# Routed expert layer: rows of two of four tiles transposed by PE, first product in two halves through three single PSUM banks, logits' bank emptied by ACT

## The chip, the cores and the metric

One core of one Trainium2 chip runs the whole program. The metric is the device time of one execution in microseconds; several executions are taken and their median counts. One further execution was recorded by the profiler, and all rows below come from it.

## The reference, cut to what matters

Three stages follow one another on 24,576 tokens (8 x 3072) of 256 channels.

```python
# 1. spectral filter along the sequence
Y = np.fft.rfft(x, axis=1) * (filt_r + 1j * filt_i)[None]
x = np.fft.irfft(Y, n=3072, axis=1).reshape(24576, 256)
# 2. routed experts, E = 8, F = 1024: each token goes through the one expert with the largest logit
for e in range(8):
    xe = x[expert_idx == e]
    out[expert_idx == e] = gate_w * (np.maximum(xe @ w1[e], 0) @ w2[e])
# 3. soft slots: 8 experts with 4 slots each
logits = out @ phi                      # 24576 x 32
d = softmax(logits, axis=0)             # over tokens
slot_input = d.T @ out                  # 32 x 256
slot_out = experts(slot_input)          # relu(s @ w1[e]) @ w2[e], 4 slots per expert
y = softmax(logits, axis=1) @ slot_out
```

## The kernel before, in words

The program has three parts that follow each other on the chip. The spectral filter (to about 760 us of the profiled span) also writes every token's row, scaled and split into two fp16 parts (high and low, 512 numbers in all) with some bookkeeping words, to a table `xd` in HBM that is sorted by expert. The routed experts (761 to 1594 us) read this table in tiles of 128 rows of one expert; there are `NT` = 199 tiles. The tail (1594 to 1718 us) works out the slots and writes the output.

The change is in the middle part, `moe_phase`. Each tile `t` passes these steps, and each engine gets them in an order that is written out by hand in `ORDER`, one loop iteration per tile, with lags (`XC` = 4 tiles, `LA` = 3, `LG` = 11):

- `load`: a DMA on ACT's queue brings the 128 rows into `mx` (line 820), six iterations ahead. Four buffers.
- `xpose`, four iterations ahead: GpSimd copies the bookkeeping words to `meta`. For tiles 0 and 1 (`PEX` = 2) PE transposes the rows by four 128x128 transposes into a PSUM tile `px`, and ACT copies it to `mxp`. For all others DVE copies the rows to `xg` (line 847), and once a pair of tiles (`XG` = 2) stands there, a DMA transpose on SP's queue writes `mxt` (line 851). Two buffers of a pair each.
- `gemm1` (line 855): 12 matmuls of 512 columns give `ph` = rows times w1 of the tile's expert, 128 x 1024 in two PSUM banks, two such buffers. The matmuls alternate between the two halves of 512 columns. ACT takes the ReLU of all 1024 columns as fp16 (line 871), then DVE takes the rest that fp16 leaves (line 872); both go to `h`. A DMA transpose on SP's queue writes `ht` (line 874).
- `l2` (line 883), three iterations later: 16 small matmuls add the tile's slot logits to `pl2`, one PSUM bank that holds the logits of four tiles (a group). There is one such bank, so the next group's first tile needs it emptied.
- `c_sum` (line 899), in the iteration after the group's last `l2`: DVE copies one half of `pl2` out (line 902) and adds the other (line 903). `c_logits`, `c_max`, `c_state`, `c_comb1`, `c_comb2`, `c_weights`, `c_low`, `c_den` follow in later iterations and make the running softmax over tokens and the softmax over slots.
- `gmm`, eleven iterations later: 8 small matmuls into a PSUM tile `pg` (two buffers), which `gacc` on DVE adds to an accumulator.

In one iteration PE's stream is: the small matmuls of the group steps, `gemm1` of tile t, `l2` of tile t-3, `gmm` of tile t-11. After the `gemm1` of every fourth tile, ahead of `l2`, PE's sequencer loads the expert numbers of the next four tiles (line 868).

PSUM has eight banks: `ph` takes four, `pg` two, `pl2` and `tr` one each.

`M1A` = 7 tiles of 512 KB of the slot experts' w1 are loaded into `m1a` during the middle part; the other 9 of 16 into `m1b` at the start of the tail (line 1087).

Of the kernel before, what the change touches and what calls it, by code (L numbers as in the profile page):

```python
# [9 lines left out]
F32 = mybir.dt.float32  # L10
F16 = mybir.dt.float16
# [3 lines left out]
AF = mybir.ActivationFunctionType  # L15
ALU = mybir.AluOpType
# [8 lines left out]
F = 1024  # L25
NS = 32
# [5 lines left out]
NT = NTOK // 128 + 7  # L32
# [3 lines left out]
R = 12  # L36
CH = 2
NEG = -1.0e30
M1A = 7
WA, WQ = 6, "G"  # L40
KW = 112
CROSS = 2
# [4 lines left out]
ENDS = (3, 3)  # L47
PF, XC, XG, XEN, XQN, XB, MEN = 6, 4, 2, "V", "SC", 4, "G"
PGB = 2
PEX = 2  # L50
LAX = 3
LGX = 8
ORDER = [('load', 0), ('weights', 4), ('state', 3), ('max', 2), ('sum', 1), ('logits', 1), ('low', 4), ('comb1', 2), ('comb2', 3), ('gacc', 0), ('den', 4), ('w2copy', 0), ('mref', 0), ('xpose', 0), ('gemm1', 0), ('l2', 0), ('gmm', 0)]
# [131 lines left out]
def build(ctx, tc, A, out):  # L185
    nc = tc.nc
    V, SC, G, PE, SY = nc.vector, nc.scalar, nc.gpsimd, nc.tensor, nc.sync
# [16 lines left out]
    w1s = cp.tile([128, E, 2, 2, F], F16, tag="big", name="w1s")  # L204
# [575 lines left out]
    def moe_phase(ctx):  # L780
        mp = ctx.enter_context(tc.tile_pool(name="mp", bufs=2))
        ps = ctx.enter_context(tc.tile_pool(name="ps2", bufs=1, space=PSUM))
# [10 lines left out]
        LG = LA + LGX  # L793
        XE, XQ = dict(V=V, G=G, SC=SC)[XEN], dict(SC=SC, SY=SY)[XQN]
        xgs = {}
        rows_, xts, metas, hs, hts, w2c, pl2s, grp, pgs, es = {}, {}, {}, {}, {}, {}, {}, {}, {}, {}


        regs = {}
# [1 line left out]
        def fetch(eng, g, f):  # L801
            if g >= NG or (id(eng), g, f) in regs:
                return
            n = min(4, NT - 4 * g)
            p, j = divmod(4 * g % 128, 32)
            _, vs = nc.values_load_multi_w_load_instructions(
                tab[p:p + 1, f, 4 * g // 128, j:j + n], engines=[eng.engine], min_val=0, max_val=(E - 1, DUMMY)[f],
                skip_runtime_bounds_check_because=why)
            regs[id(eng), g, f] = vs

        def val(eng, j, f):
            fetch(eng, j // 4, f)
            return regs[id(eng), j // 4, f][j % 4]
# [10 lines left out]
        def xpose(t):  # L824
            if t >= NT:
                return
            x = rows_.pop(t)
            g, q = divmod(t, 4)
            if q == 0:
                metas[g] = mp.tile([128, 4, 4], F32, tag="meta", name=f"meta{g}", bufs=6)  # L830
            (V if MEN == "V" else G).tensor_copy(metas[g][:, q, :], x[:, 512:PITCH].bitcast(F32))
            if t == NT - 1 and q < 3:
                V.memset(metas[g][:, q + 1:], 0.0)
                V.memset(metas[g][:, q + 1:, 1:2], NEG)
            if t < PEX:

                px = ps.tile([128, 4, 128], F16, tag="pg", name=f"px{t}", bufs=PGB)
                for k in range(4):
                    PE.transpose(px[:, k, :], x[:, k * 128:k * 128 + 128].bitcast(F16), id16)
                xt = mp.tile([128, 4, 128], F16, tag="xt", name=f"mxp{t}", bufs=2)  # L840
                SC.copy(xt, px)
                xts[t] = xt
                return
            g, q = divmod(t, XG)
            if q == 0:
                xgs[g] = mp.tile([128, XG, 512], F16, tag="xg", name=f"xg{g}", bufs=2)
            (XE.copy if XE is SC else XE.tensor_copy)(xgs[g][:, q, :].bitcast(U16), x[:, 0:512])
            if q == XG - 1 or t == NT - 1:
                xg = xgs.pop(g)
                xt = mp.tile([128, XG * 4, 128], F16, tag="xt", name=f"mxt{g}", bufs=2)  # L850
                SY.dma_start_transpose(out=xt[:, 0:4 * q + 4], in_=xg[:, 0:q + 1].rearrange("p a f -> p (a f)"))
                for i in range(q + 1):
                    xts[t - q + i] = xt[:, 4 * i:4 * i + 4]

        def gemm1(t):
            e = val(PE, t, 0)
            ph = ps.tile([128, F], F32, tag="ph", name=f"ph{t}", bufs=2)
            xt = xts.pop(t)
            n = [0, 0]
            for k in range(2):  # L860
                for part, ws in ((0, (0, 1)), (1, (0,))):
                    for w in ws:
                        for hf in range(2):
                            PE.matmul(ph[:, hf * 512:hf * 512 + 512], xt[:, 2 * part + k, :],  # L864
                                      w1s[:, ds(e, 1), k, w, hf * 512:hf * 512 + 512].rearrange("p a f -> p (a f)"),
                                      start=(n[hf] == 0), stop=(n[hf] == 5))
                            n[hf] += 1
            if t % 4 == 2:
                fetch(PE, t // 4 + 1, 0)
            h = mp.tile([128, 2, F], F16, tag="h", name=f"h{t}", bufs=LG + 2)  # L870
            SC.activation(h[:, 0, :], ph, AF.Relu)  # L871
            V.scalar_tensor_tensor(out=h[:, 1, :], in0=ph, scalar=0.0, in1=h[:, 0, :], op0=ALU.max, op1=ALU.subtract)  # L872
            ht = mp.tile([128, 16, 128], F16, tag="ht", name=f"ht{t}", bufs=LA + 1)
            SY.dma_start_transpose(out=ht, in_=h.rearrange("p a f -> p (a f)"))
            hs[t], hts[t] = h, ht
# [7 lines left out]
        def l2(t):  # L883
            g, q = divmod(t, 4)
            if q == 0:
                pl2s[g] = ps.tile([128, 4, 2 * NS], F32, tag="pl2", name=f"pl2_{g}")
            ht, w = hts.pop(t), w2c.pop(t)
            for k in range(8):
                PE.matmul(pl2s[g][:, q, :], ht[:, k, :], w[:, k, :], start=(q == 0 and k == 0), stop=False, skip_group_check=True)  # L889
                PE.matmul(pl2s[g][:, q, 0:NS], ht[:, 8 + k, :], w[:, k, 0:NS], start=False, stop=((q == 3 or t == NT - 1) and k == 7),  # L890
                          skip_group_check=True)

        n4 = [128, 4, NS]
        b4 = lambda v: v.unsqueeze(2).to_broadcast(n4)
# [4 lines left out]
        def c_sum(g):  # L899
            a = n4t("a", g)  # L900
            m = min(4, NT - 4 * g)
            V.tensor_copy(a[:, 0:m], pl2s[g][:, 0:m, NS:])
            V.tensor_tensor(out=a[:, 0:m], in0=a[:, 0:m], in1=pl2s[g][:, 0:m, 0:NS], op=ALU.add)
            if m < 4:
                V.memset(a[:, m:], 0.0)
            grp[g] = dict(a=a)
# [125 lines left out]
        for t in range(XC):  # L1032
            xpose(t)
            if t + XB < PF:
                load(t + XB)
        for t in range(NT + LG + 2):
            if t >= 16 and t % 8 == 0 and t < 16 + 8 * M1A:
                SY.dma_start(m1a[:, t // 8 - 2, :], w21[t // 8 - 2])
            if t == NT:
                w, get = weights("moe_w2", C, "w2n")  # L1040
                w2n.extend(w)
                get(SY, range(WA))
            ops = dict(weights=c_weights, state=c_state, max=c_max, sum=c_sum, logits=c_logits, low=c_low, comb1=c_comb1, comb2=c_comb2,
                       den=c_den)
            one = dict(gacc=(gacc, LG + 1), w2copy=(w2copy, LA - 1), mref=(mref, LG), xpose=(xpose, -XC), gemm1=(gemm1, 0), l2=(l2, LA), gmm=(gmm, LG), load=(load, -PF))
            for n_, lag in ORDER:
                if n_ in one:
                    at(t, one[n_][0], one[n_][1])
                else:
                    grp_at(t, ops[n_], lag)  # L1050
# [20 lines left out]
    def weights(src, n, nm):  # L1071
        w = cp.tile([128, E, A[src].shape[1] // 128, n], F32, tag="big", name=nm)
        return [w[:, e] for e in range(E)], lambda q, es: [
            q.dma_start(w[:, e], A[src][e].rearrange("(k p) c -> p k c", p=128)) for e in es
        ]

    w2n = []
    m1a = cm.tile([128, M1A, F], F32, tag="m1a", name="m1a")
    w21 = A["moe2_w1"].rearrange("e (k p) f -> (e k) p f", p=128)


    def tail(ctx):
        tp = ctx.enter_context(tc.tile_pool(name="tp", bufs=1))
        ps = ctx.enter_context(tc.tile_pool(name="ps3", bufs=1, space=PSUM))
        m1b = tp.tile([128, 2 * E - M1A, F], F32, tag="big", name="m1b")
        for i in range(M1A, 2 * E):
            SY.dma_start(m1b[:, i - M1A, :], w21[i])
        m1 = [m1a[:, i] if i < M1A else m1b[:, i - M1A] for i in range(2 * E)]
        M = sm.tile([128, 1], F32, tag="M", name="M")
# [123 lines left out]
    with ExitStack() as c3:  # L1213
        moe_phase(c3)
# [31 lines left out]
```

## Time and profile before

| | us |
|---|---|
| median of 3 executions | 1716.07 (1710.61 to 1718.2) |
| the profiled execution, its own time | 1719.86 |
| its span, first to last instruction | 1718.1 |
| PE busy | 1449.7 (84% of the span) |
| DVE busy | 1203.3 (70%) |
| ACT busy | 784.7 (46%) |
| GpSimd busy | 636.9 (37%) |

The profiled execution took 3.8 us more than the median of the others, and 1.8 us of its time lie outside the span. A matmul's end is modelled in these rows, so that several matmuls overlap; the distance between two starts tells how fast PE goes. The idle time printed with a group is what its engine lay idle just before its instructions, and the arrow names what ended the wait.

### The profile page before, as it was taken

The page shows a single profiled execution, that of the slowest core. Times are in us where ns is not written, and L with a number is a line of the kernel's source. Part 1 is how long each engine was busy: PE and PEld are TensorE (multiplying, and loading weights), DVE is VectorE, ACT ScalarE, POOL GpSimd, SP SyncE. Part 2 cuts the span into 40 slices and gives each one's busy share as a digit, 9 for nine tenths or more (in the row PEclk, how much of TensorE's full clock was granted, in tenths as well). Part 3 has the DMA queues.
Part 4 walks back from the last instruction along what each step waited for, and adds up shares of the span by engine and source line. Part 5 has one row for each costly group of instructions (what it writes and reads, how often), then busy time and mean ns, then how long its engine had stood idle before and what let it go on. Part 6 is the DMA issues. An engine that isn't in the chain of part 4 may idle for free.

```text
span 1718.1 us, 35843 instructions
## 1 busy us (share of the span) xinstructions
PE 1449.7 (84%) x10761; PEld 682.8 (40%) x10761; DVE 1203.3 (70%) x3053; ACT 784.7 (46%) x1816; POOL 636.9 (37%) x877
## 2 busy tenths in 40 slices
PE   6768779988888876648999989999999999997876
PEld 2222224333444433324444444544444444443332
DVE  0377779999999955445677777877777777776134
ACT  3355436554666655423444444444444444443133
POOL 1122224665566644531333333333333333334200
PEclk9898989999999987769999999999999999997899
DMA  8999989997878665439999999999999999999999
GB/s 284 296 318 309 288 263 298 292 280 221 252 241 250 207 220 186 160 113 207 205 212 227 202 201 207 211 202 200 211 199 197 207 200 203 204 200 249 337 313 376
DMA packets 720696, 405.72 MB, mean 236 GB/s; under 512 B 554561, under 2 KB 658896, under 8 KB 720512
## 3 DMA queue, kind: packets, MB, share of 16 engines
q1 hardware_dynamic: 634560, 295.09, 77.4%
q10 hardware_dynamic: 69824, 77.52, 15.2%
q0 software_dynamic: 16128, 30.83, 5.5%
q8 instruction: 95, 1.56, 0.4%
q14 instruction: 89, 0.73, 0.1%
HBM read 164.60 MB, written 105.52 MB: 157 GB/s over the span
## 4 chain that ended last, share of the span: by engine, by line
PE 38%; DVE 23%; DMA 17%; ACT 9%; issue 8%; another core or an unknown queue 3%; ACTq 1%; SPq 1%; POOL 0%; DVEq 0%
PE ph L864 13%; DVE h L872 5%; DMA ht<-h 5%; ACT h L871 4%; PE p L440 3%; PE U L363 3%; PE W L331 2%; DVE rows L468 2%; DMA vd<-vo 2%; PE pl L889 2%; PE p L307 2%; DMA zd<-zo 2%; PE pg L1000 2%; DMA mxt<-xg 2%
## 5 line engine op out<-in xcount | busy, mean ns | idle before, releaser
L864 PE MATMUL ph<-w1s,mxt 128*128 x2364 | 547.4, 381 | 10.2 <-DMA mxt<-xg 6.7
L864 PEld LDWEIGHTS <-mxt 128*128 128x128 f16 x2364 | 232.4, 101 | 264.2 <-issue 26.1
L872 DVE SCALAR_TENSOR_TENSOR h<-ph,h 128x1024 f16<-128x1024 f32 x199 | 243.2, 1222 | 123.4 <-ACT h L871 106.9
L871 ACT ACTIVATE h<-ph 128x1024 f16<-128x1024 f32 x199 | 203.5, 1022 | 163.6 <-PE ph L864 115.1
L404 POOL DMA_INDIRECT xd<-rows,dest x192 | 189.5, 987 | 160.2 <-ACT xT L478 51.7
L388 POOL TENSOR_TENSOR t<-t,t 112x512 f32<-112x512 f32 x112 | 142.0, 1271 | 251.8 <-DVE t L385 237.1
L935 POOL DMA_INDIRECT cd<-cr,meta x199 | 196.9, 989 | 62.4 <-issue 47.2
L363 PE MATMUL U<-zi,mt 96*128 96x512 f32 x256 | 146.6, 657 | 41.2 <-issue 20.3
L889 PE MATMUL pl<-w2c,ht 128*128 128x64 f16 x1592 | 114.9, 190 | 44.7 <-DVE fl L911 21.9
L331 PE MATMUL W<-t,mt 112*96 112x512 f32 x288 | 151.1, 617 | 0.8 <-ACT vo L332 0.8
L889 PEld LDWEIGHTS <-ht 128*128 128x128 f16 x1592 | 101.9, 97 | 83.6 <-issue 37.5
L307 PE MATMUL p<-xt,cs 128*128 128x512 f32 x192 | 114.1, 689 | 21.4 <-DMA xt<-in_x 11.6
L440 PE MATMUL p<-vt,cs 128*128 128x512 f32 x192 | 113.5, 675 | 18.1 <-DVE rows L468 17.9
L890 PE MATMUL pl<-w2c,ht 128*128 128x32 f16 x1592 | 112.2, 178 | 0.0
L478 ACT COPY xT<-tr 128x1024 f16<-128x1024 f16 x96 | 97.0, 1010 | 29.1 <-remote 16.2
L462 ACT ACTIVATE rows<-p,r 128x256 f16<-128x256 f32 x192 | 80.6, 472 | 64.4 <-DVE r L459 38.2
L332 ACT COPY vo<-W 96x512 f32<-96x512 f32 x128 | 74.4, 581 | 71.1 <-PE W L331 50.6
L890 PEld LDWEIGHTS <-ht 128*128 128x128 f16 x1592 | 95.5, 96 | 25.2 <-issue 12.2
L1015 DVE TENSOR_TENSOR acc<-acc,pg 128x512 f32 x149 | 101.6, 682 | 1.5 <-PE pg L1004 0.7
L309 ACT COPY zo<-p 128x512 f32<-128x512 f32 x96 | 55.9, 582 | 93.7 <-PE p L307 51.6
L380 DVE TENSOR_TENSOR t<-U,w2s 112x512 f32<-112x512 f32 x128 | 87.8, 686 | 15.5 <-PE U L363 6.9
L477 PEld LDWEIGHTS <-rows 128*128 128x128 f16 x768 | 56.2, 105 | 93.6 <-issue 93.6
(246 smaller groups left out, 2151.5 us busy)
## 6 DMA issues: line engine op xcount, KB each, us to landing
mx<-xd ACTq DMA_DIRECT2D x199, 130.0 KB
xt<-in_x SPq DMA_DIRECT2D x96, 256.0 KB
zd<-zo ACTq DMA_DIRECT2D x96, 256.0 KB
zi<-zd SPq DMA_DIRECT2D x128, 192.0 KB
vd<-vo ACTq DMA_DIRECT2D x128, 192.0 KB
vt<-vd SPq DMA_DIRECT2D x96, 256.0 KB
out_y<-ot SPq DMA_DIRECT2D x48, 512.0 KB
w2s<-in_ff SPq DMA_DIRECT2D x93, 96.0 KB
```

Source lines behind the costliest of these rows:

```text
L307: PE.matmul(p, cs1[:, 0:128], xt[:, 2 * m:2 * m + 2, :], start=True, stop=True)
L331: PE.matmul(W, mt[:, 128 + 96 * i:224 + 96 * i], t, start=(i == 0), stop=(i == len(ts) - 1))
L363: PE.matmul(U, mt[0:96, 0:128], zi, start=True, stop=True)
L388: G.tensor_tensor(out=t1, in0=t1, in1=t2, op=ALU.add)
L404: i = G.indirect_dma_start(out=xd, out_offset=bass.IndirectOffsetOnAxis(ap=dest[:, t:t + 1], axis=0), in_=rows[:, t % 2, :].bitcast(U16), ...
L440: PE.matmul(p, cs1[:, 128:256], vt[:, 2 * i % CH:2 * i % CH + 2, :], start=True, stop=True)
L864: PE.matmul(ph[:, hf * 512:hf * 512 + 512], xt[:, 2 * part + k, :], w1s[:, ds(e, 1), k, w, hf * 512:hf * 512 + 512].rearrange("p a f -> p ...
L871: SC.activation(h[:, 0, :], ph, AF.Relu)
L872: V.scalar_tensor_tensor(out=h[:, 1, :], in0=ph, scalar=0.0, in1=h[:, 0, :], op0=ALU.max, op1=ALU.subtract)
L889: PE.matmul(pl2s[g][:, q, :], ht[:, k, :], w[:, k, :], start=(q == 0 and k == 0), stop=False, skip_group_check=True)
L890: PE.matmul(pl2s[g][:, q, 0:NS], ht[:, 8 + k, :], w[:, k, 0:NS], start=False, stop=((q == 3 or t == NT - 1) and k == 7), skip_group_check= ...
L935: i = G.indirect_dma_start(out=cd, out_offset=bass.IndirectOffsetOnAxis(ap=metas[g].bitcast(U32)[:, q, 2:3], axis=0), in_=cr[:, q].rearran ...
```

## The change

- Tiles with `t % 4` of 0 or 1 are transposed by PE (four transposes into `px`, now a PSUM bank of its own, then an ACT copy to one of three `xp` buffers). The other two of four go by DVE copy and DMA transpose as before.
- `gemm1` makes the first 512 columns with six matmuls and then the other 512, each half in a PSUM bank of its own out of three. ACT's ReLU and DVE's rest run on each half. The DMA transpose of `h` still waits for both.
- After the last `l2` of a group ACT copies the whole `pl2` bank to an SBUF tile `plc`. `c_sum` is one DVE addition that reads `plc`; the DVE copy goes.
- `M1A` is 6: one tile of w1 more is loaded in the tail.

PSUM is then: `ph` three banks, `px` one, `pg` two, `pl2` one, `tr` one.

```diff
-M1A = 7
+M1A = 6
-PEX = 2
@@ xpose
-            if t < PEX:
-                px = ps.tile([128, 4, 128], F16, tag="pg", name=f"px{t}", bufs=PGB)
+            if t % 4 < 2:
+                px = ps.tile([128, 4, 128], F16, tag="px", name=f"px{t}")
                 for k in range(4):
                     PE.transpose(px[:, k, :], x[:, k * 128:k * 128 + 128].bitcast(F16), id16)
-                xt = mp.tile([128, 4, 128], F16, tag="xt", name=f"mxp{t}", bufs=2)
+                xt = mp.tile([128, 4, 128], F16, tag="xp", name=f"mxp{t}", bufs=3)
                 SC.copy(xt, px)
@@ gemm1
-            ph = ps.tile([128, F], F32, tag="ph", name=f"ph{t}", bufs=2)
             xt = xts.pop(t)
-            n = [0, 0]
-            for k in range(2):
-                for part, ws in ((0, (0, 1)), (1, (0,))):
-                    for w in ws:
-                        for hf in range(2):
-                            PE.matmul(ph[:, hf * 512:hf * 512 + 512], xt[:, 2 * part + k, :],
-                                      w1s[:, ds(e, 1), k, w, hf * 512:hf * 512 + 512].rearrange("p a f -> p (a f)"),
-                                      start=(n[hf] == 0), stop=(n[hf] == 5))
-                            n[hf] += 1
+            h = mp.tile([128, 2, F], F16, tag="h", name=f"h{t}", bufs=LG + 2)
+            for hf in range(2):
+                f = slice(hf * 512, hf * 512 + 512)
+                ph = ps.tile([128, 512], F32, tag="ph", name=f"ph{t}{hf}", bufs=3)
+                n = 0
+                for k in range(2):
+                    for part, ws in ((0, (0, 1)), (1, (0,))):
+                        for w in ws:
+                            PE.matmul(ph, xt[:, 2 * part + k, :], w1s[:, ds(e, 1), k, w, f].rearrange("p a f -> p (a f)"),
+                                      start=(n == 0), stop=(n == 5))
+                            n += 1
+                SC.activation(h[:, 0, f], ph, AF.Relu)
+                V.scalar_tensor_tensor(out=h[:, 1, f], in0=ph, scalar=0.0, in1=h[:, 0, f], op0=ALU.max, op1=ALU.subtract)
             if t % 4 == 2:
                 fetch(PE, t // 4 + 1, 0)
-            h = mp.tile([128, 2, F], F16, tag="h", name=f"h{t}", bufs=LG + 2)
-            SC.activation(h[:, 0, :], ph, AF.Relu)
-            V.scalar_tensor_tensor(out=h[:, 1, :], in0=ph, scalar=0.0, in1=h[:, 0, :], op0=ALU.max, op1=ALU.subtract)
@@ l2, at its end
+            if q == 3 or t == NT - 1:
+                plc[g] = mp.tile([128, 4, 2 * NS], F32, tag="plc", name=f"plc{g}", bufs=1)
+                SC.copy(plc[g][:, 0:q + 1], pl2s.pop(g)[:, 0:q + 1])
@@ c_sum
-            V.tensor_copy(a[:, 0:m], pl2s[g][:, 0:m, NS:])
-            V.tensor_tensor(out=a[:, 0:m], in0=a[:, 0:m], in1=pl2s[g][:, 0:m, 0:NS], op=ALU.add)
+            V.tensor_tensor(out=a[:, 0:m], in0=plc[g][:, 0:m, NS:], in1=plc[g][:, 0:m, 0:NS], op=ALU.add)
```

## Rows read from the trace of the kernel before

**Rows 1.** Busy time by stretch; columns: stretch, length, engines' busy time, clock, DMA share, GB/s.
```profile
761.00:1594.00 833.00, 766.60 (x7378) 382.56 (x7378) 616.51 (x1605) 355.63 (x1101) 292.85 (x552) 0.98 1.15 205
1594.00:1718.00 124.00, 97.53 (x572) 39.38 (x570) 40.13 (x65) 35.09 (x39) 7.62 (x9) 0.91 1.00 351
```

**Rows 2.** Group of the first product, 761 to 1594 us, PE: busy, mean ns, idle before.
```profile
L864 PE MATMUL ph<-w1s,mxt 128*128 x2364 | 547.4, 381 | 10.2 <-DMA mxt<-xg 6.7 <-issue 3.0
```

**Rows 3.** Waits of PE, 761 to 1594 us: total, times, longest.
```profile
PE pl L889 <- DVE fl L911: 21.9, 32, 3.1
PE pl L889 <- DMA ht<-h: 11.7, 13, 1.6
PE ph L864 <- DMA mxt<-xg: 6.7, 7, 1.8
```

**Rows 4.** Timeline of PE, 1101 to 1120 us: start, length, what.
```profile
1103.43 2.76 PE L864 MATMUL ph<-w1s,mxt 128*128 x12
...
1106.56 0.19 PE L889 MATMUL pl<-w2c,ht 128*128 128x64 f16 x1 [0.36 <-DVE fl L911]
...
1107.68 2.75 PE L864 MATMUL ph<-w1s,mxt 128*128 x12
...
1111.47 2.75 PE L864 MATMUL ph<-w1s,mxt 128*128 x12
...
1115.18 2.75 PE L864 MATMUL ph<-w1s,mxt 128*128 x12
...
1118.73 1.47 PE L864 MATMUL ph<-w1s,mxt 128*128 x6
```

**Rows 5.** Timeline of all engines, 1102 to 1108 us, around the logits' bank.
```profile
1102.88 0.18 PE L890 MATMUL pl<-w2c,ht 128*128 128x32 f16 x1
...
1104.83 0.34 ACTq L820 DMA_DIRECT2D mx<-xd  x1
1105.80 0.29 DVE L902 COPY a<-pl 128x128 f32<-128x128 f32 x1 [0.85 <-remote]
```

**Rows 6.** Timeline of PE, 437 to 439 us: transposes of the filter stage.
```profile
437.77 0.61 PE L477 MATMUL tr<-id,rows 128*128 128x128 f16 x8
438.22 0.35 PE L496 MATMUL misc<-wgs,xT 128*128 128x16 f16 x8
```

**Rows 7.** Groups by line, shapes apart or by stretch: busy, mean ns, idle before.
```profile
L871 ACT ACTIVATE h<-ph 128x1024 f16<-128x1024 f32 x199 | 203.5, 1022 | 163.6 <-PE ph L864 115.1 <-PE pg L1004 15.9 <-remote 13.9
L872 DVE SCALAR_TENSOR_TENSOR h<-ph,h 128x1024 f16<-128x1024 f32 x199 | 243.2, 1222 | 123.4 <-ACT h L871 106.9 <-issue 14.0 <-ACT mst L1019 1.1
L468 DVE SCALAR_TENSOR_TENSOR rows<-p,r,rows 128x256 f16<-128x256 f32 x192 | 86.4, 478 | 2.1 <-ACT rows L462 0.8 <-issue 0.3
L462 ACT ACTIVATE rows<-p,r 128x256 f16<-128x256 f32 x192 | 80.6, 472 | 64.4 <-DVE r L459 38.2
L841 ACT COPY mxp<-px 128x512 f16<-128x512 f16 x2 | 1.2, 585 | 6.1 <-DVE rg L217 4.1 <-POOL meta L831 2.1
```

**Rows 8.** Timeline of SP's queue, 1000 to 1030 us: DMA issues.
```profile
1013.00 1.25 SPq L851 DMA_TRANSPOSE mxt<-xg  x1
1014.34 4.99 SPq L874 DMA_TRANSPOSE ht<-h  x2
1019.49 1.86 SPq L851 DMA_TRANSPOSE mxt<-xg  x1
1021.45 7.41 SPq L874 DMA_TRANSPOSE ht<-h  x2
```

**Rows 9.** The chain that ended last, 1015 to 1045 us.
```profile
1034.14 8.28 DMA ht<-h
```

**Rows 10.** Timeline, 774 to 783 us: a row load and who waited.
```profile
777.77 0.36 ACTq L820 DMA_DIRECT2D mx<-xd  x1
...
781.82 0.19 POOL L831 COPY meta<-mx 128x4 f32<-128x4 f32 x1 [3.44 <-DMA mx<-xd]
```

**Rows 11.** Timeline, 1590 to 1637 us: SP's queue in the tail.
```profile
1593.15 7.40 SPq L1087 DMA_DIRECT2D m1b<-in_moe_w  x9
```

More of the change, by code (lines that the diff above doesn't have):

```diff
@@ L795, in moe_phase @@
         xgs = {}
-        rows_, xts, metas, hs, hts, w2c, pl2s, grp, pgs, es = {}, {}, {}, {}, {}, {}, {}, {}, {}, {}
+        rows_, xts, metas, hs, hts, w2c, pl2s, plc, grp, pgs, es = {}, {}, {}, {}, {}, {}, {}, {}, {}, {}, {}
         regs = {}
```

## The prediction

> **What bounds the kernel now.** I read the busy time by stretch first [rows 1]. The change lies in the stretch from 761 to 1594 us, apart from one DMA of the tail. There PE is busy 766.6 of 833 us, DVE 616.5, ACT 355.6: PE sets the pace, and about 66 us of it are idle by this count. The reader is to see next, in the timeline of PE, what a tile costs when nothing holds it [rows 4]: the first product starts at 1107.68, 1111.47, 1115.18 and 1118.73, so 3.79, 3.71 and 3.55 us a tile. The tile before took 4.25, because the logits' matmuls waited for the bank that DVE had to empty. The waits of PE name three causes [rows 3]: the logits' bank (21.9 us in 32 waits), the transposed `ht` (11.7 in 13) and the transposed rows `mxt` (6.7 in 7).
>
> These counts are too small. A matmul is shown with 381 ns [rows 2], but twelve take 2.75 us [rows 4], so starts are (2.75 - 0.38) / 11 = 0.215 us apart, and the first 0.17 us of each wait hide under the shown end of the matmul before. With 0.17 us for each, the three waits cost 27.3, 13.9 and 7.9 us, 49 in all.
>
> Behind the two DMA waits stands SP's queue, which issues the transposes: 1.25 + 4.99 + 1.86 + 7.41 = 15.5 us of issuing in the 15.9 us from 1013.00 to 1028.86, for four tiles [rows 8]. A tile's `ht` takes 8.28 us from issue to use in the chain [rows 9], of about 11 us that three tiles give it.
>
> **The change part by part.**
>
> *PE's transposes, added.* Tiles with `t % 4` below 2 are 100 of 199, of which two went this way already: 98 x 4 = 392 transposes. The trace has the same instruction in the filter stage: eight start at 437.77, what follows at 438.22 [rows 6], so 0.056 us each while PE runs without a break; with the shown length, 0.61 us for eight, it would be 0.076. The bounds are 22 and 30 us. I take the lower, since here too matmuls follow at once, and 0.03 us a tile for getting in and out: 25 us. This is on the path, because PE sets the pace. The Trainium skill (TensorE: Matmul & The Clock Gate, Part 4: PE-mode transpose) speaks against it: such a transpose took about 275 ns in one kernel's context. By that the 392 would cost 108 us; these rows show a fifth of it.
>
> *The row loads are now waited for by PE.* Behind a late one stand all of PE's matmuls, and DVE and ACT behind these. The load for a PE tile is issued in the iteration two before its transposes. The tightest of a group is issued at 1104.83 [rows 5], in the iteration whose product starts at 1103.43, and PE would want it just ahead of 1111.47 [rows 4]: 6.6 us. Early in the stage one takes 781.82 - 777.77 = 4.05 us [rows 10], so it is covered by 2.5 us. The change moves this very issue back (below) to about 1106.3, which leaves 5.1 us against 4.05. I take no wait; without that cover each us late costs 1 us in one tile of four, 50 us in all.
>
> *DMA transposes, removed.* 49 of 99 `mxt` issues go, one per four tiles: 1.25 to 1.86 us of the 15.5. The pairs that stay have twice the time until their buffer is needed again. I take all of the `mxt` wait as gone: 7.9 us.
>
> *The first product in halves.* The matmuls are the same twelve. ACT's half costs about 0.585 us, the copy of 128x512 from PSUM, and DVE's lies between 478 ns for 256 columns and 1222 for 1024 [rows 7], 0.73 us on a straight line. `h` is then complete 0.585 + 0.73 = 1.3 us after the last matmul instead of 1.02 + 1.22 = 2.2, so `ht` is issued up to 0.9 us sooner, into a queue with one issue less in four tiles. Against that the three tiles that it has get shorter by some 0.2 us. Of 13.9 us I take 11 as gone; the bounds are 0 and 13.9. The work itself grows: ACT by 199 x 0.15 = 30, 98 x 0.585 = 57 for `px` and 50 x 0.47 = 24 for the logits, 111 us to 467 of 833; DVE by at most 199 x 0.23 = 46 to 662 of 833, before its dropped copies are taken off. Both stay hidden under PE. With three banks, the second half of tile t+1 needs the first half of tile t emptied, and starts about 3.7 us after that was made; ReLU and rest take 1.3 of them. If ACT and DVE came 0.7 us too late in one tile of four, that would be 35 us. I take nothing.
>
> *The logits' bank emptied by ACT.* In the clean case the last matmul of the group ends at 1102.88 + 0.18 = 1103.06, but DVE's copy starts only at 1105.80 after idling 0.85 us [rows 5]: it waits 2.7 us for a signal, and its releaser is not told ("remote"). It comes in the iteration where PE's sequencer loads the next expert numbers; I suppose that it comes as late for ACT. PE could have gone on at 1103.43 + 12 x 0.215 = 1106.01 and went at 1106.56. ACT's copy of 128x256 lies near the 0.47 us of the row of that size [rows 7] and needs no second instruction: with 0.14 us until PE starts it frees the bank at 1105.8 + 0.47 + 0.14 = 1106.4 at worst, 0.4 us late, or on time if ACT has the signal and copies sooner. I take 0.2 us left per group, 10 us in 50 groups: 27.3 - 10 = 17 us gain, bounds 7 and 27. Where DVE itself is behind (the longest wait is 3.1 us [rows 3]) it helps most. The price stands on ACT's queue: behind the copy wait the next row load, the small copies and the next ReLU, some 1.5 us once in four tiles.
>
> *Tail.* One DMA of 512 KB joins nine that are issued from 1593.15 on [rows 11]; at the stretch's 351 GB/s [rows 1] it takes 1.5 us. PE first does the sums and their matmuls, so I take nothing and keep 1.5 as the bound.
>
> *Sum.* 7.9 + 11 + 17 - 25 = 11 us gained. The profiled execution would go from 1719.9 to 1709, and the median, 3.8 us below it, from 1716 to 1705.
>
> **The rivals.**
>
> *Better: the DMA side held more than its named waits.* SP's queue is issuing 98% of the time [rows 8]. If all three waits go, and some of the 66 us idle that has no name (66 - 40 = 26) with them, it is 49 + 10 - 22 = 37 us: 1679, and 49 - 22 = 27 us without these: 1689. For: the queue. Against: three of four tiles run at PE's own pace already [rows 4].
>
> *No gain: the bank's wait stays.* ACT gets the same late signal, its copy is 0.4 us late in each group, and ACT's longer queue gives back what the halves won for `ht`: 7 + 8 - 25 is 10 us lost, 1726, and 1719 if half of the `ht` wait goes.
>
> *Slower: PE waits for the row load.* The load behind ACT's copy has 5.1 us. If it lands in 6.1, and `ht` takes 8.3 under the same load [rows 9], PE loses 1 us in every group, 50 us: 1753. It decides from a landing time of 5.1 us on. Against: the transposes are four times as large and queue behind each other.
>
> *Slower: the third bank.* The 35 us from above: 1738.
>
> *Slower: a transpose is as dear as an isolated one.* If each took five times the 0.056 us, 83 us more: 1786. The Trainium skill's figure above comes to this.
>
> **How the numbers follow.** Chances: as summed 0.46 (own range 1695 to 1712), better 0.22 (1677 to 1692), no gain 0.16 (1713 to 1728), late row load 0.09, third bank 0.05, dear transposes 0.02. A measurement of this kernel tells about 0.5%, 8.6 us, from no change. Faster by more: seven tenths of the first and all of the second, 0.54. Within it: the rest of the first and seven tenths of the third, 0.25. Slower: the rest, 0.21. The range 1678 to 1728 holds the first three cases and leaves out the last three.
>
> **What would show it.** PE's 392 more transposes at 0.056 us between starts; the product's starts 3.6 to 4.0 us apart, with 0.25 more where transposes stand; the logits' wait at 0.2 us a group and on ACT instead of DVE; waits for `mxt` gone, for `ht` under 3 us. I am wrong if PE waits for `mx` before its transposes, if the second half's first matmul waits for DVE, or if ACT's copy of the logits comes later than 3.3 us after the group's last matmul.

## The result, and the profile after

The changed kernel took 1735.2 us (median of 4 runs, 1730.06 to 1740.12) against 1713.3 us before (4 runs, 1710.43 to 1718.2; the chip of this first pair is not on record): a ratio of 1.0124, 95% interval 1.0084 to 1.0165. It became 1.2% slower. I had predicted 1705 us and left 21 in 100 for slower. The profiled execution took 1730.1 us, 10.2 more than that of before, which lies 6.5 above its median; the new one lies 5 below its own.

The busy time by stretch, as in [rows 1]:

```profile
761.00:1594.00 833.00, 779.26 (x7708) 409.32 (x7707) 588.66 (x1630) 430.47 (x1426) 287.21 (x544) 0.99 1.00 185
1594.00:1728.00 134.00, 102.75 (x626) 41.63 (x626) 47.23 (x84) 38.90 (x60) 13.82 (x18) 0.89 1.02 357
```

The DMA engines are relieved (share 1.00 for 1.15). In the trace, the first product of the stage starts at 765.8 and the last at 1575.4 us, before at 763.2 and 1563.9: 809.6 for 800.6 us. So 9 of the 10.2 us between these two executions arise in the stage of the change; the medians lie 21.9 us apart. PE's waits there (total, times, longest), which answer to [rows 3]:

```profile
PE pg L1005 <- issue: 22.5, 34, 0.9
PE ph L865 <- DVE h L869: 6.1, 9, 0.8
PE pg L1001 <- issue: 5.8, 10, 0.9
PE px L838 <- DMA mx<-xd: 3.2, 1, 3.2
...
PE pl L888 <- DMA ht<-h: 2.5, 2, 1.3
...
PE pl L888 <- ACT plc L893: 1.6, 2, 1.2
```

All three waits of before are gone or small, as predicted: the logits' bank 21.9 to 1.6, `ht` 11.7 to 2.5, `mxt` from 6.7 to nothing. But 28 us now stand at a place that had 2.0, **in the middle of `gmm`** (L1001, L1005), with no releaser: "issue" is time in which PE waited for nothing that the profile shows. The timeline of all engines in one step with `t % 4 == 2`, as in [rows 4] and [rows 5], shows it:

```profile
1114.69 1.03 POOL L936 DMA_INDIRECT cd<-cr,meta  x1 [0.30 <-POOL cr L934]
...
1115.86 0.33 PE L981 MATMUL pb<-c,pT 128*128 128x128 f32 x1
...
1116.02 2.75 PE L865 MATMUL ph<-w1s,mxt 128*128 x12
1116.03 0.97 POOL L936 DMA_INDIRECT cd<-cr,meta  x1 [0.30 <-issue]
...
1117.31 0.97 POOL L936 DMA_INDIRECT cd<-cr,meta  x1 [0.30 <-issue]
...
1118.58 0.98 POOL L936 DMA_INDIRECT cd<-cr,meta  x1 [0.30 <-issue]
...
1119.02 0.29 DVE L983 TENSOR_TENSOR v<-pb,fg 128x128 f32<-128x128 f32 x1 [2.60 <-PE ph L865]
...
1119.36 0.27 PE L1005 MATMUL pg<-h,vs 128*32 128x256 f16 x1
...
1120.48 0.34 PE L1005 MATMUL pg<-h,vs 128*32 128x256 f16 x3 [0.85 <-issue]
...
1120.56 0.60 ACT L868 ACTIVATE h<-ph 128x512 f16<-128x512 f32 x1 [0.83 <-PE pl L889]
```

`pb` leaves PE at 1116.19, and DVE, idle, reads it at 1119.02. ReLU of the half product that ends at 1117.48 (six matmuls 0.215 us apart and 0.38 for the last) starts at 1120.56, after ACT has idled for 0.83 us. Signals come some 3 us late, for DVE and ACT alike, while GpSimd issues the group's four indirect DMAs. And PE itself stops for 1.1 us between two matmuls that wait for nothing.

From start to start of the product, over the 49 whole groups, the steps with `t % 4` = 1, 2, 3, 0 take 3.66, 4.57, 4.15 and 3.98 us on average in the changed kernel and 3.85, 3.82, 4.54 and 3.98 in that of before: 16.37 and 16.19 us a group. In the changed kernel the step of the stall costs 0.75 us more; the next one, where before waited for the logits' bank, costs 0.4 less.

### The profile page after: what moved, and what is told of

Its sections match the earlier page's. It is cut to its first block, busy times and chain, and to the rows that moved or that the text cites. A ratio compares the mean times of both kernels' runs of the same rounds, so it can differ in the third digit from the quotient of the medians.

```text
span 1728.3 us, 36779 instructions
## 1 busy us (share of the span) xinstructions
PE 1471.4 (85%) x11153; PEld 709.9 (41%) x11153; DVE 1182.8 (68%) x3104; ACT 864.3 (50%) x2163; POOL 639.0 (37%) x877
## 4 chain that ended last, share of the span: by engine, by line
PE 59%; DVE 15%; DMA 14%; issue 6%; ACT 4%; another core or an unknown queue 1%; ACTq 0%; POOL 0%; SPq 0%; DVEq 0%; POOLq 0%
PE ph L865 28%; PE U L362 3%; PE pg L1001 3%; PE pl L888 3%; PE p L439 3%; PE W L330 3%; DMA zd<-zo 2%; DMA out_y<-ot 2%; DVE rows L467 2%; PE p L306 2%; PE pg L1005 2%; PE pl L889 2%; DMA vd<-vo 2%; DMA wt<-in_moe_w 2%; PE tr L476 1%
## 5 line engine op out<-in xcount | busy, mean ns | idle before, releaser
L869 DVE SCALAR_TENSOR_TENSOR h<-ph,h 128x512 f16<-128x512 f32 x398 | 264.9, 687 | 75.6 <-ACT h L868 65.6
L868 ACT ACTIVATE h<-ph 128x512 f16<-128x512 f32 x398 | 231.6, 595 | 116.5 <-PE ph L865 74.6
L865 PE MATMUL ph<-w1s,mxt 128*128 x1188 | 275.5, 379 | 8.9 <-DVE h L869 6.1
L865 PE MATMUL ph<-w1s,mxp 128*128 x1200 | 276.4, 380 | 0.4 <-issue 0.4
L362 PE MATMUL U<-zi,mt 96*128 96x512 f32 x256 | 150.1, 672 | 34.8 <-issue 11.8
L865 PEld LDWEIGHTS <-mxt 128*128 128x128 f16 x1188 | 114.8, 100 | 139.1 <-issue 19.7
L865 PEld LDWEIGHTS <-mxp 128*128 128x128 f16 x1200 | 113.6, 98 | 119.5 <-issue 2.2
L889 PEld LDWEIGHTS <-ht 128*128 128x128 f16 x1592 | 95.9, 96 | 26.7 <-issue 3.7
L985 ACT CAST vs<-v 128x128 f16<-128x128 f32 x50 | 14.9, 298 | 178.9 <-DVE v L983 78.0
L983 DVE TENSOR_TENSOR v<-pb,fg 128x128 f32<-128x128 f32 x50 | 14.6, 291 | 128.7 <-PE ph L865 94.0
```

What stands on the lines that cost most here:

```text
L362: PE.matmul(U, mt[0:96, 0:128], zi, start=True, stop=True)
L865: PE.matmul(ph, xt[:, 2 * part + k, :], w1s[:, ds(e, 1), k, w, f].rearrange("p a f -> p (a f)"), start=(n == 0), stop=(n == 5))
L868: SC.activation(h[:, 0, f], ph, AF.Relu)
L869: V.scalar_tensor_tensor(out=h[:, 1, f], in0=ph, scalar=0.0, in1=h[:, 0, f], op0=ALU.max, op1=ALU.subtract)
```

## The experiments

The runs came in nine groups on nine chips, each with its own runs of the kernel before beside it. On eight of them the kernel before took 1667 to 1673 us; on one, chip 14, 1719 us, as in the first pair. This turned out to be the main finding, so each is told with its chip.

**First group, chip 7 (before 1670.0 us).** Theory S blames GpSimd's four DMAs, theory R the PE sequencer's register load of that step.

`a1_spread` takes the row of DMAs apart:

```diff
-            for q in range(min(4, NT - 4 * g)):
-                i = G.indirect_dma_start(
...
+            d.update(cr=cr)
+
+        def scat(t):
+            g, q = divmod(t, 4)
+            i = G.indirect_dma_start(
...
+            one = dict(scat=(scat, LA + 6), gacc=(gacc, LG + 1), ...
```

> The changed kernel with the four indirect DMAs of a group issued one a tile instead of four in a row. Theory S (the four in a row on GpSimd, 4.9 us, hold back the signals of all engines, and PE's stall of 1.1 us in each step t%4 = 2 is their effect): signals are late by under 1 us instead of 3, the step of t%4 = 2 falls from 4.6 to about 3.7 us, 49 groups x 0.9 us = 45 us faster than the changed kernel, 1680 to 1700 us. Theory R (TensorE's register load in that step does it): nothing changes, 1735 us within 8, the late signals stay in step t%4 = 2.

`a1_loadmoved`:

```diff
-            if t % 4 == 2:
+            if t % 4 == 0:
                 fetch(PE, t // 4 + 1, 0)
```

> The changed kernel with TensorE's register load in the step t%4 = 0 instead of t%4 = 2. Theory S: the stall stays in the step t%4 = 2 at about 1.1 us and the time at 1735 us within 8. Theory R: the stall and the late signals move to the step t%4 = 0, two steps on; the time may stay, the place may not.

`a1_nopex`:

```diff
-            if t % 4 < 2:
+            if t < 0:
```

> The changed kernel without its transposes on PE (all tiles go through the DMA transpose as before; halves, single banks and ACT's copy stay). By the prediction's terms 25 us of transposes leave the path and 7.9 us of waits for transposed rows come back: 1735 - 17 = 1718 us. If the transposes were what cost the 21 us and more (a dearer transpose, waits for rows): below 1713 us. If the stall of step t%4 = 2 grows out of the transposes, it is gone here; by theories S and R it stays at about 1 us.

`b1_plc` is the kernel before with the third part of the change alone (`plc` by ACT, M1A = 6).

> The kernel before with the logits' bank emptied by ACT alone, the third part of the change. By the prediction's step the wait of 21.9 us for that bank falls to 5: 1713 - 17 = 1696 us. By theory S or R the signal that lets ACT copy is as late as the one that let DVE read; only the shorter emptying (0.38 us for 0.29 + 0.29) is left, 0.2 to 0.3 us a group, 1698 to 1705 us, unless PE's wait for the signal turns up elsewhere in the same step: then 1713 us within 6.

Measured, as ratios to the kernel before: `a1_spread` 0.9726 (0.9697 to 0.9754), `a1_loadmoved` 0.9744 (0.972 to 0.9769), `a1_nopex` 0.9989 (0.9966 to 1.0011), `b1_plc` 0.9975 (0.9953 to 0.9997). The first two both gained 2.6 to 2.7%, and in neither trace was there a stall. That neither theory had foreseen for both, and `a1_nopex` and `b1_plc`, which keep DMAs and load as they were, had no late signals either. So the changed kernel itself had to be run beside them.

**Second group, chip 8 (before 1666.9 us):** the changed kernel and that of before as they are, and `b2_spread`, the spread DMAs in the kernel before.

> The changed kernel as it is, as the control for the first four runs: there the kernel before took 1670 us, and no signal was late in any of the four. Theory H (the late signals belong to the execution, not to the program: where a signal comes at once, the changed kernel's group takes its floor of 15.22 us): about 1625 us where before takes 1670, 2.7% faster, no stall in step t%4 = 2. Theory P (the program makes them: only spreading the indirect DMAs or moving the register load takes them away): about 1.1 us x 49 = 50 us above the spread kernel, 1675 us where before takes 1670, the stall of 1.1 us in every step t%4 = 2.

> The kernel before, for its trace beside the other runs of this chip. Theory H: signals of all engines within 0.1 us of their instruction's end in every step, and PE's wait for the logits' bank well under the 21.9 us of the first trace. Theory P: signals 2 to 3 us late in the steps t%4 = 2, as in the first trace.

> The kernel before with the four indirect DMAs of a group issued one a tile. Theory H: no difference, within 0.5% of the kernel before, if signals come at once there; theory P (by the four in a row): 20 us or more faster than before, since the wait of 21.9 us for the logits' bank goes.

`c_after`: 1622.3 us, ratio 0.9738 (0.971 to 0.9765). Theory H was right. On this chip the changed kernel as it is is **2.6% faster** than before. `b2_spread`: 0.9962 (0.9938 to 0.9987), `c_before` 1659.3 in its one run. The same step on this chip, in `c_after`:

```profile
1011.59 1.03 POOL L936 DMA_INDIRECT cd<-cr,meta  x1 [0.30 <-POOL cr L934]
...
1012.75 0.33 PE L981 MATMUL pb<-c,pT 128*128 128x128 f32 x1
...
1012.92 2.75 PE L865 MATMUL ph<-w1s,mxt 128*128 x12
...
1013.23 0.28 DVE L983 TENSOR_TENSOR v<-pb,fg 128x128 f32<-128x128 f32 x1
...
1016.03 0.40 PE L1001 MATMUL pg<-h,vs 128*32 128x512 f16 x4
...
1016.25 0.28 PE L1005 MATMUL pg<-h,vs 128*32 128x256 f16 x4
```

The DMAs run at the same place and as long, but DVE reads `pb` 0.48 us after its transpose starts (3.16 in the first trace), and `gmm` runs through.

I counted in the traces every instruction of PE, DVE, ACT and GpSimd that raises its engine's semaphore, whether the rise came more than 0.5 us after its end, and whether that fell near a row of indirect DMAs (from 0.5 us ahead of it to 2.5 us past its end):

```
kernel, chip               signals   late   of them near indirect DMAs
before, first pair            5644    718    718
changed, first pair           6291    837    837
c_before, chip 8              5644     24     24
c_after, chip 8               6291     22     22
e_before_load4, chip 14       5644    759    759
e_after_load4, chip 14        6291    785    785
```

Under half of all signals (2498 of 5644 in the first) are near such DMAs, but every late one is. (Not every rise is recorded, and fewer are where signals are late, so the late counts there shift by 3 to 6% with the way they are matched to instructions.) In the first trace the first late one comes at 320 us and the last at 1592; GpSimd's indirect DMAs run from 311 to 1592 us, from the filter stage on. The first product of the kernel before starts at 763 us there and at 717 on chip 8. Round a group's four DMAs the longest stretch without any engine's signal has a median of 2.5 us in the changed kernel of the first pair and 0.63 on chip 8.

Where signals come in time, PE's waits in the product stage show what the change removes; the two largest of `c_before` (717 to 1510 us), then those of `c_after` (717 to 1473 us):

```profile
PE pl L889 <- DMA ht<-h: 26.7, 27, 3.1
PE ph L864 <- DMA mxt<-xg: 8.5, 12, 1.6
```

```profile
PE pl L888 <- DMA ht<-h: 2.4, 3, 1.3
PE px L838 <- DMA mx<-xd: 2.1, 1, 2.1
```

And SP's queue in `c_before`, which is hardly ever idle:

```profile
1089.03 1.29 SPq L851 DMA_TRANSPOSE mxt<-xg  x1
1090.42 5.10 SPq L874 DMA_TRANSPOSE ht<-h  x2
1095.68 1.91 SPq L851 DMA_TRANSPOSE mxt<-xg  x1
1097.68 6.72 SPq L874 DMA_TRANSPOSE ht<-h  x2
1104.57 1.24 SPq L851 DMA_TRANSPOSE mxt<-xg  x1
```

From 1089.03 to 1104.57 it issues 15.0 of 15.5 us for one group. Over 640 us the issues fill 94% in `c_before` and 82% in `c_after`, 93% and 74% in the first pair.

**Third group, chip 0 (before 1670.0 us):** which part gains. `b3_pex` is the kernel before with PE's transposes alone:

```diff
-            if t < PEX:
+            if t % 4 < 2:
...
-                xt = mp.tile([128, 4, 128], F16, tag="xt", name=f"mxp{t}", bufs=2)
+                xt = mp.tile([128, 4, 128], F16, tag="xp", name=f"mxp{t}", bufs=3)
```

> The kernel before with the PE transposes of two tiles in four alone (the product whole in its two double banks, the logits' bank emptied by DVE; the transposes take turns in gmm's two banks; the m1a buffer one shorter). Theory D (where signals come at once, what holds the kernel before is the queue of DMA transposes: PE waits 31 us for ht and 7 for mxt in 720 us, and half the row transposes leave that queue): most of the gain comes with this part alone, 1635 us within 10 where before takes 1667. Theory E (it takes the halves too, since ht waits for h, and h comes 0.9 us sooner by them): 1650 to 1667 us.

`a2_noplc` takes the third part out of the changed kernel:

```diff
-                SC.copy(plc[g][:, 0:q + 1], pl2s.pop(g)[:, 0:q + 1])
...
-            V.tensor_tensor(out=a[:, 0:m], in0=plc[g][:, 0:m, NS:], in1=plc[g][:, 0:m, 0:NS], op=ALU.add)
+            V.tensor_copy(a[:, 0:m], pl2s[g][:, 0:m, NS:])
+            V.tensor_tensor(out=a[:, 0:m], in0=a[:, 0:m], in1=pl2s[g][:, 0:m, 0:NS], op=ALU.add)
```

> The changed kernel with the logits' bank emptied by DVE in two reads as before. Theory D: with signals in time nothing waits for that bank, 1625 us within 6 where the changed kernel takes 1622. By the prediction's step 17 us of wait for the bank come back: 1640 us.

`d_plain`:

```diff
-                i = G.indirect_dma_start(
...
+                SC.dma_start(cd[t * 128:t * 128 + 128, :], grp[g]["cr"][:, q].rearrange("p r s -> p (r s)"))
```

> The changed kernel with the 199 indirect DMAs on GpSimd left out of the product stage; in their place one plain DMA a tile from ACT's queue writes the tile's weights into rows in order (192 of 199 tiles), so the last stage reads wrong rows. Where signals come at once: the same as the changed kernel within 8 us (1622 where before takes 1667), since no engine waits for GpSimd there. Where they come late as in the first pair of traces: theory S has no late signal left in the product stage and 1735 falls to 1670 to 1690; theory R leaves the stall of 1.1 us in each step t%4 = 2.

`b3_pex` 0.9766 (0.9735 to 0.9797), `a2_noplc` 0.9728 (0.9697 to 0.9759), `d_plain` 0.9708 (0.9673 to 0.9742). The transposes alone bring 2.3 of the 2.6%; the bank's copy by ACT brings nothing where signals are in time; and nothing waits for GpSimd's DMAs there. Together with `a1_nopex` (no transposes, no gain) theory D stands. PE's waits for `ht` go with this part, first `a1_nopex` (724 to 1515 us), then `b3_pex` (717 to 1480 us):

```profile
PE pl L888 <- DMA ht<-h: 27.1, 26, 2.5
```

```profile
PE pl L889 <- DMA ht<-h: 2.6, 3, 1.5
```

A rival is that the part helps because DVE is spared half of its row copies. The traces speak for the queue: from the end of DVE's last work on `h` to the issue of `ht`'s transpose there pass 2.13 us on average in `c_before`, 1.16 in `a1_nopex` and 0.30 in `b3_pex` (800 to 1440 us).

**Fourth group, chip 14 (before 1719.1 us):** late signals again. Both kernels were to have three more register loads in the step `t % 4 == 2`:

```diff
...
             if t % 4 == 2:
                 fetch(PE, t // 4 + 1, 0)
+                again(t // 4 + 1, 3)
```

> The changed kernel with TensorE's register load of the step t%4 = 2 done four times in a row (the three added values are not used). It holds PE's sequencer longer, as the late load of the first traces did (3.5 us from the load to the next address computed, against 1.95 us where signals come at once). Theory R' (PE's queue of matmuls already handed over lasts some 2 to 2.5 us after the load; what the sequencer is held beyond that is a stall in gmm): with 3 loads more, 1 to 3 us, a stall of 0.5 to 2 us a group, 25 to 100 us slower than the changed kernel (1622 where before takes 1667), and it sits between gmm's matmuls. If the sequencer's hold is not what stalls PE: 1622 within 6.

> The kernel before with the same three register loads added. Theory D (a group lasts 15.9 us there because of six DMA transposes in SP's queue, PE has about 1.2 us of waiting a group): the first 1.2 us of the stall are hidden under the waits for ht and mxt, so it loses at least 30 us less than the changed kernel does, 0 to 40 us slower than before. If the stall added is not hidden: as much slower as the changed kernel becomes.

The trace shows that the loads, unused, were dropped in compiling; what stayed is three instructions a group on PE's sequencer that raise a semaphore (147 in all, 0.05 us each, 0.15 apart). So this is a test of three more signals, not of loads. `e_after_load4` took 1754.9 us, 1.0203 (1.0153 to 1.0253), against 1.0124 (1.0084 to 1.0165) for the changed kernel in the first pair; from the first product's start to the last one's it takes 826.5 us for 809.6, 17 us more. `e_before_load4` is 1.0027 (0.9998 to 1.0056), with 795.7 us for 800.6. PE's waits of `e_after_load4` (L1011 and L1015 are `gmm`, L898 and L899 the logits' matmuls, 768 to 1600 us):

```profile
PE pg L1015 <- issue: 15.1, 23, 1.0
PE ph L874 <- DVE h L878: 14.5, 22, 1.0
PE pg L1011 <- issue: 12.2, 15, 1.4
PE pl L899 <- issue: 6.1, 8, 1.2
PE pl L898 <- issue: 3.8, 8, 0.7
```

The unnamed stall is longer (37 us for 28) and begins earlier in the step, in `gmm`'s first half and the logits' matmuls; the wait at the third bank has grown too, from 6.1 to 14.5 us. That the changed kernel feels three more signals is likely but not shown: it did not run without them on this chip, and its interval touches that of the first pair. The kernel before loses at most 0.6% by them. In its waits, too, the bank and the DMA stand side by side:

```profile
PE pl L899 <- DVE fl L921: 12.1, 22, 1.3
PE pl L899 <- DMA ht<-h: 11.9, 12, 2.4
```

**Later groups.** To separate S from R where signals are late, the first two versions were run again, and all fell on chips without late signals: chips 10, 12, 2, 11 and 9 (before 1667.9, 1668.1, 1670.1, 1669.5, 1673.1 us).

> The changed kernel with the four indirect DMAs of a group issued one a tile, once more, for a chip where before takes 1713 to 1720 us. Theory S: no stretch of 2.5 us without a signal, the step t%4 = 2 falls from 4.6 to 3.6 us and the time from 1735 to 1690 us within 10. Theory R: the stall follows the register load if a DMA still falls on it: 1715 to 1735 us. Where before takes 1667 us nothing is late and it takes 1623.

> The changed kernel with TensorE's register load in the step t%4 = 0, two tiles away from the four indirect DMAs, for a chip where before takes 1713 to 1720 us. Theory R: PE's sequencer is no longer held, the stall between gmm's matmuls goes, 4.6 to 3.6 us in that step, 1735 to 1690 us within 10, although the signals stay late. Theory S alone (late signals to ACT and DVE stall PE by themselves): 1735 within 8. Where before takes 1667 us it takes 1623.

> The changed kernel with TensorE's register load in the step t%4 = 0, for a chip where before takes 1713 to 1720 us. Theory R (the load's late return holds PE's sequencer and empties PE's queue in gmm): the step t%4 = 2 falls from 4.6 to 3.6 us, 1735 to 1690 us within 10, with the signals as late as before. Theory S alone (late signals to ACT and DVE stall PE by themselves): 1735 us within 8. Where before takes 1667 us it takes 1623.

> The changed kernel with TensorE's register load in the step t%4 = 0, for a chip where before takes 1713 to 1720 us. Theory R (the load's late return holds PE's sequencer and empties PE's queue in gmm): the step t%4 = 2 falls from 4.6 to 3.6 us, 1735 to 1690 us within 10, with the signals as late as before. Theory S alone (late signals to ACT and DVE stall PE by themselves): 1735 us within 8. Where before takes 1667 us it takes 1623.

> The changed kernel with the four indirect DMAs of a group issued one a tile, for a chip where before takes 1713 to 1720 us. Theory S (the four in a row make the signals late): no stretch of 2.5 us without a signal in the product stage, the step t%4 = 2 falls from 4.6 to 3.6 us and the time from 1735 to 1690 us within 10. If the late signals have another cause: 1735 within 8, late in the same steps. Where before takes 1667 us nothing is late and it takes 1623.

> As for the run before: on a chip where before takes 1713 to 1720 us, theory S gives 1690 us within 10 and a step t%4 = 2 of 3.6 us; another cause gives 1735 within 8. Where before takes 1667 us nothing is late and it takes 1623.

Spread (`f_`, `i_`, `j_`): 0.9721, 0.973, 0.9717. Load moved (`f_`, `g_`, `h_`): 0.976, 0.9761, 0.972. The intervals lie between 0.967 and 0.982, and all hold `c_after`'s 0.9738. They say nothing on S or R; what they show is that versions of the changed kernel gain 2.4 to 2.8% on every chip here where signals are in time.

## Why the prediction was wrong

**The step that failed: the gain of 17 us from the logits' bank.** I saw that DVE's copy there came 2.7 us after the last matmul, took all of this as waiting for a signal, and priced it as a delay of that bank alone, to be shortened by a shorter copy. Of these 2.7 us DVE idled for only 0.85 [rows 5] and 0.29; in between it worked, most of it on `h`, as this line of the kernel before shows:

```profile
1103.73 1.23 DVE L872 SCALAR_TENSOR_TENSOR h<-ph,h 128x1024 f16<-128x1024 f32 x1 [0.29 <-issue]
```

On chip 8 its copy, too, starts 1.81 us after the group's last matmul (median), and no wait of PE is put down to that bank there. ACT's copy was nearly as late as I supposed, in the median 2.25 us after the group's last matmul (0.10 on chip 8), and the wait did vanish, 21.9 to 1.6 us. But the late signal was no property of the bank: in that stretch the signals of all engines come late, and PE now stalls elsewhere in it or just behind it, 28 us without a named cause in `gmm` (all 44 times with `t % 4 == 2`) and 6 us at the third bank, which I had put at nothing. So the three waits of 49 us were replaced by waits of about the same size (48 us counted in the same way), and PE's transposes came on top. That makes a loss of some 21 us; between the two traces the stage lost 9, since smaller waits outside this sum shrank, from 29 to 12 us in these views.

**Why before hardly felt it.** Two things limit a group there: six DMA transposes in SP's queue, 15.5 us, and PE with its stalls. On chip 8, with hardly a late signal, the stage of before takes 789.6 us, 15.96 a group; in the first pair, 800.6 and 16.19. Most of what late signals cost PE was made up for, since PE then waited less for `ht` (11.7 us for 26.7 in `c_before`). The changed kernel has no such slack: its stage takes 750.1 us on chip 8, 15.15 a group, with under 6 us of waits, and 809.6 us, 16.37 a group, in the first pair. So the stage of the changed kernel is 59.5 us longer in the first pair, where signals are late, than on chip 8, and that of before 11.0. The difference, 48.5 us, makes of the 39.5 us gained on chip 8 the 9.0 us lost in the first pair.

**PE's transposes, 25 us: right.** On chip 8 the steps that hold four transposes are 0.22 us longer (3.79 to 4.01), 2 x 0.22 x 49 = 22 us; starts are 0.055 us apart. The Trainium skill (TensorE: Matmul & The Clock Gate, Part 4: PE-mode transpose) has about 275 ns for one in one kernel's context. As the length of one this is not far from the traces, which show 0.219 us; but with matmuls ahead and behind the starts lie a fifth of the 275 ns apart, and that is what PE pays here.

**Row loads, 0: right.** PE waits once for `mx`, 3.2 us at the start of the stage.

**`mxt` 7.9 and `ht` 11: right in place,** and with the "better" rival's reason. Where signals are in time these two are most of what PE waits for (35 of 43 us in `c_before`). With them gone the product stage shrinks from 789.6 to 750.1 us on chip 8. The rival had 37 us gained, for SP's queue at 98%; 44 were measured there. I gave it 0.22, because three of four tiles ran at PE's pace in the window that I read; over the stage 103 of 184 do (within 0.1 us). The three rivals on the slow side (1753, 1738, 1786) are added to 1703 where my sum gives 1705; nothing hangs on these 2 us.

**Third bank, 0: nearly.** 6.1 us in 9 waits of the second half's first matmul, all in the step behind the stall; none on chip 8. I had named such a wait as a sign of being wrong. **ACT and DVE, hidden: right.** ACT came to 430 us (predicted 467), DVE to 589 (at most 662); a half takes ACT 0.597 and DVE 0.687 us. **Tail, 0: right** within what the traces tell: the last product's start to the end of the span is 152.9 us for 154.2.

**What stays open.** That GpSimd's indirect DMAs make the signals late is shown by coincidence only: every late signal is near them, in the first pair and on chip 14 (perhaps the first pair's own), and beside the same DMAs hardly one is late on eight others. Neither a spread nor a leave-out fell on a chip with late signals. Nor did a kernel with one part of the change alone, so which part meets the late signals is not shown. How PE comes to stop between matmuls that wait for nothing is open too. In 40 groups of the changed kernel in the first pair, PE's sequencer computed the next addresses at a median of 4.35 us into the step (2.78 on chip 8), so the register load's late return fits many groups; but in 17 of the 40 they were computed before 3.25 us, and 14 of these steps still took over 4.5. The longer and earlier stall beside three more signals would fit signals that pile up undelivered, but does not prove it. And why chips differ in this no run tells.

## What to carry to other kernels

Ask of each late signal whether other engines' signals are late in the same stretch: then it belongs to the stretch, and a change that removes the wait may only hand it to the next instruction. A wait hidden behind another bound costs little until that bound is lifted (here the late signals' 11 us became 59.5); the change that lifts it must be priced with the wait in full. And measure the kernel before on more than one chip when a verdict hangs on 1 or 2%: here one says 1.2% slower and another 2.6% faster, of the same two programs.

## What the hardware showed that was not expected

The kernel before takes 1713 us in the first pair and 1719 on chip 14, but 1667 to 1673 on eight other chips, with the same instruction times (`pb`'s transpose 0.33 us, an indirect DMA's issue 0.97, half a product's ReLU 0.60 in both) and about the same granted clock (0.938 and 0.949). The difference that the traces show is in when signals arrive: 13% of them over 0.5 us late on the one kind, 0.4% on the other. For the kernel before, 47 of the 61 us between the two profiled spans (1718.1 and 1657.5) lie ahead of the first product, not in the product stage. Up to GpSimd's first indirect DMA the two traces run level (311 and 312 us).
